# Rebuilding the end of attention and the batch norm of a conformer block

## The chip, the cores and the metric

The kernel runs on one core of one Trainium2 chip. The metric is the device time of one execution in microseconds (us). Most executions of a kernel agree within 0.3%; a change counts as faster or slower here from 2% on. The profile and the trace come from one profiled execution of each kernel; their clock starts at the span's first instruction. "Span" is the time from the first to the last instruction, some 4 us less than the device time.

## The reference

A conformer block on 2 x 4000 tokens of 512 features, bf16 inputs: feed-forward, attention, gated depthwise convolution with a batch norm over all 8000 tokens, second feed-forward, with a layer norm ahead of each and one at the end.

```python
    h = _layernorm(x, axis=-1)
    h = _silu(h @ w_ff1_a) @ w_ff1_b
    x1 = x + 0.5 * h
    ...                                        # layer norm, q, k, v
    attn = jnp.einsum('bts,bsd->btd', p, v) @ w_o
    x2 = x1 + attn
    h = _layernorm(x2, axis=-1)
    h = h @ w_pw1
    h = a * _sigmoid(b)                        # a, b: the two halves
    ...                                        # dc: depthwise, 3 taps over time
    mu = flat.mean(0)                          # over all tokens of both batches
    var = ((flat - mu) ** 2).mean(0)
    dc = (dc - mu[None, None, :]) / jnp.sqrt(var[None, None, :] + 1e-05)
    h = _silu(dc) @ w_pw2
    x3 = x2 + h
    h = _layernorm(x3, axis=-1)
    h = _silu(h @ w_ff2_a) @ w_ff2_b
    x4 = x3 + 0.5 * h
    return _layernorm(x4, axis=-1)
```

The batch norm is what makes a seam: no token can go on before the last token's convolution is counted.

## The kernel before

Tokens are worked in 16 chunks of 500, each four tiles of 125. The first feed-forward of all chunks, attention of all chunks and the second feed-forward of all chunks follow each other, and TensorE is full in each. The convolution of chunks 0 to 12 is done beside attention. Between attention and the second feed-forward lies the seam: chunk 15's projection and layer norm, the gates of chunks 14 and 15, the depthwise convolutions of chunks 13 to 15 (as matmuls with diagonal matrices), the batch norm's factors, and a start of the second feed-forward.

A layer norm takes bn_stats (statistics) of each tile, then aggregates, adds eps, and takes the power -1/2 on GpSimd for all four tiles together:

```python
    def ln_aggr(self, c, sl, shift=False):
        for ti in range(TPC):
            S.op("DVE", lambda e, ti=ti: e.bn_aggr(self.mv[sl][:, ti, :], self.st[sl][:, ti, :]), ...)
        S.op("DVE", lambda e: e.tensor_scalar(self.va[sl], self.mv[sl][:, :, 1], EPS, None, ALU.add), ...)
        S.op("POOL", lambda e: e.tensor_tensor(out=self.rs[sl], in0=self.va[sl],
                                               in1=self.neghalf[0:TILE, :], op=ALU.pow), ...)
```

The seam, cut:

```python
        gate = [f for jj in range(DC) for f in (lambda jj=jj: self.conv_b(tail, jj), lambda jj=jj: self.conv_a(tail, jj))]
        for ti in range(TPC):
            gate.pop(0)()
            self.project(last, ti)             # attention's projection, and the residual on VectorE
            self.ln_stats(last, sl, ti)
        self.ln_aggr(last, sl)
        ...
        for ti in range(TPC):
            self.ln_norm(last, sl, ti, ..., "DVE")
        self.transposes_pe(1, ("DVE", "DVE"))  # four banks, four copies
        ...
        for jj in range(DC):                   # four blocks of 128 channels of chunk 15
            self.conv_b(last, jj)
            self.conv_a(last, jj)
            ...                                # depthwise, then finish(): statistics over all 16 chunks
        ...
        for t in range(2):
            for cc in range(DC):
                self.swish(t, cc)
        self.warm(16)                          # 16 matmuls whose result nobody reads
        banks = [self.sbank() for _ in all_t]
        self.pw2(0, all_t, banks)              # second pointwise of chunk 0
        for ti in all_t:
            self.pw2_residual(0, [ti], banks[ti:ti + 1])
            self.ln_stats(0, sl, ti)
        self.ln_aggr(0, sl)
        ...
        self.pw2_sum(1, all_t, ybanks)         # chunks 1 and 2: 40 matmuls beside the layer norm
        self.pw2_sum(2, all_t, [self.sbank() for _ in all_t])
        for ti in all_t:
            self.ln_norm(0, sl, ti, ..., "DVE")
        for ti in all_t:
            self.transpose_pe(ti, 0, ("DVE", "ACT")[ti % 2], ybanks[ti])
```

## Time and profile before

| | before |
|---|---|
| device time, median of 3 | 2066.26 us (2066.22 to 2067.23) |
| span of the profiled run | 2061.7 us |
| TensorE (PE) busy | 2049.0 us, 99% |
| VectorE (DVE), ScalarE (ACT), GpSimd (POOL) busy | 54%, 36%, 6% |
| the seam, from the row sums to the first matmul of the second feed-forward | 1524.21 to 1572.74, 48.53 us |

PEld is TensorE's weight load, which overlaps its matmuls. The lines of the profile, and what follows from them, are in the prediction below. DVE, ACT and POOL are the profile's names for VectorE, ScalarE and GpSimd.

### The profile page before, as it was taken

How to read it: one execution, taken by the hardware profiler on the slowest of the kernel's cores; microseconds unless marked ns; L12 is line 12 of the kernel's file. 1: busy time of each engine (PE TensorE's matmuls, PEld its weight loads, DVE VectorE, ACT ScalarE, POOL GpSimd, SP SyncE). 2: the span in 40 equal slices, each digit the busy share in tenths (PEclk: the TensorE clock that was granted, in tenths of full speed). 3: DMA queues.
4: the chain of work that ended last, by engine and by line, in shares of the span. 5: the costliest groups of instructions: out<-in, count | busy, mean ns of one | idle time of the engine just before them, and what ended most of it. 6: DMA issues, size and time to landing. Idle time of an engine off the chain costs nothing.

```text
span 2061.7 us, 24361 instructions
## 1 busy us (share of the span) xinstructions
PE 2049.0 (99%) x9642; PEld 1038.6 (50%) x9644; DVE 1104.3 (54%) x2252; ACT 745.1 (36%) x1271; POOL 130.1 (6%) x271
## 2 busy tenths in 40 slices
PE   9999999999999999999999999999999999999998
PEld 4555555554444444444444444444445555555554
DVE  4244444325556667666666666666764434434443
ACT  3433333333333333333333333333336433443432
POOL 2011100000000000000000000000010000000000
PEclk9999999999999999999999999999999999999999
DMA  7222221110000100014301010001143111111111
GB/s 178 56 61 53 60 61 49 46 49 11 16 6 23 24 16 21 19 23 113 92 13 24 18 23 16 21 18 24 55 111 92 31 31 40 32 31 40 32 31 42
DMA packets 209324, 87.73 MB, mean 43 GB/s; under 512 B 157873, under 2 KB 208692, under 8 KB 209204
## 3 DMA queue, kind: packets, MB, share of 16 engines
q1 hardware_dynamic: 208808, 85.79, 16.9%
q8 instruction: 78, 1.28, 0.3%
q14 instruction: 42, 0.34, 0.1%
q10 hardware_dynamic: 396, 0.31, 0.0%
HBM read 29.53 MB, written 19.04 MB: 24 GB/s over the span
## 4 chain that ended last, share of the span: by engine, by line
PE 98%; DVE 1%; ACT 1%; issue 0%; POOL 0%; POOLq 0%; ACTq 0%
PE s L463 55%; PE y L463 42%; DVE wff L976 0%; ACT work L493 0%; DVE work L552 0%; ACT keys L493 0%; DVE wff L910 0%; ACT wff L493 0%; DVE work L485 0%; DVE xt L634 0%; DVE work L529 0%; DVE work L983 0%; POOL work L539 0%; PE s L478 0%; DVE work L715 0%
## 5 line engine op out<-in xcount | busy, mean ns | idle before, releaser
L493 ACT ACTIVATE work<-s 128x500 bf16<-128x500 f32 (+2 forms) x1063 | 623.9, 587 | 1220.8 <-PE s L463 1218.3
L463 PE MATMUL s<-work,wff 128*128 128x500 bf16 x2560 | 627.7, 376 | 1.4 <-ACT work L493 0.8
L463 PE MATMUL s<-work,keys 128*128 128x500 bf16 x2048 | 517.5, 374 | 0.1
L463 PE MATMUL y<-work,keys 128*128 128x500 bf16 x2048 | 514.4, 373 | 0.1
L463 PE MATMUL y<-wff,work 128*125 128x512 bf16 x2016 | 506.6, 379 | 0.0
L786 DVE TENSOR_TENSOR work<-work 128x500 f32<-128x500 f32 x496 | 334.9, 675 | 287.9 <-ACT work L493 285.3
L463 PEld LDWEIGHTS s<-work,wff 128*128 128x128 bf16 x2560 | 250.1, 98 | 280.4 <-issue 1.7
L463 PEld LDWEIGHTS y<-wff,work 128*125 128x125 bf16 x2016 | 275.2, 137 | 173.5
L463 PEld LDWEIGHTS y<-work,keys 128*128 128x128 bf16 x2048 | 199.2, 97 | 234.4 <-DVE work L851 1.1
L463 PEld LDWEIGHTS s<-work,keys 128*128 128x128 bf16 x2048 | 199.8, 98 | 232.2 <-DVE work L715 0.6
L634 DVE SCALAR_TENSOR_TENSOR xt<-y,xt 125x512 bf16<-125x512 f32 x128 | 79.8, 684 | 352.4 <-PE y L463 352.4
L529 DVE BATCH_NORM_STATS2 work<-xt 125x6 f32<-125x512 bf16 x320 | 202.5, 681 | 10.4 <-DMA xt<-in_x_dram 10.0
L539 POOL TENSOR_TENSOR work<-work 125x4 f32<-125x4 f32 x78 | 79.2, 1015 | 1122.0 <-DVE work L537 1122.0
L463 PE MATMUL s<-work 128*125 128x512 bf16 (+3 forms) x544 | 138.7, 380 | 2.4 <-DVE work L1091 1.3
L552 DVE TENSOR_SCALAR work<-xt,work 125x512 bf16<-125x512 bf16 x285 | 113.2, 442 | 19.8 <-POOL work L539 16.4
L634 DVE SCALAR_TENSOR_TENSOR xt<-s,xt 125x512 bf16<-125x512 f32 x56 | 38.7, 691 | 141.6 <-PE s L463 141.6
L463 PEld LDWEIGHTS s<-work 128*125 128x125 bf16 (+2 forms) x544 | 72.5, 135 | 51.2 <-issue 5.4
L634 DVE SCALAR_TENSOR_TENSOR xt<-s,work,xt 125x512 bf16<-125x512 f32 x64 | 48.1, 751 | 32.8 <-PE s L463 32.2
L463 PE MATMUL s<-keys,work 128*128 128x500 bf16 x256 | 64.4, 376 | 0.0
L914 DVE SCALAR_TENSOR_TENSOR wff<-wff,s 128x500 bf16<-128x500 f32 x56 | 38.0, 678 | 42.2 <-PE s L463 40.2
L493 ACT ACTIVATE wff<-s 128x500 f32<-128x500 f32 x68 | 39.9, 587 | 54.3 <-PE s L463 52.2
L961 POOL COPY wff<-wff 128x1 bf16<-128x1 bf16 x56 | 10.5, 188 | 636.4 <-DVE wff L914 626.8
(79 smaller groups left out, 518.5 us busy)
## 6 DMA issues: line engine op xcount, KB each, us to landing
xt<-in_x_dram SPq DMA_DIRECT2D x15, 500.0 KB
out_dram<-work SPq DMA_DIRECT2D x15, 500.0 KB
dcvd<-wff SPq DMA_DIRECT2D x52, 125.0 KB, 1.7
keys<-dcvd SPq DMA_DIRECT2D x13, 500.0 KB, 4.5
wff<-in_w_ff_a_dram SPq DMA_DIRECT2D x16, 256.0 KB, 4.2
keys<-work SPq DMA_DIRECT2D x8, 512.0 KB, 3.6
keys<-keys SPq DMA_DIRECT2D x32, 128.0 KB, 2.1
work<-work SPq DMA_TRANSPOSE x210, 2.5
```

Source lines behind the costliest of these rows:

```text
L463: self.S.op("PE", lambda e: e.matmul(out, lhsT, rhs, start=start, stop=stop), reads=reads, writes=[bank], inc=stop if inc is None else inc)
L493: return self.S.op("ACT", lambda e: e.activation(out, in_, func, **kw), reads=reads, writes=writes)
L529: self.S.op("DVE", lambda e: e.bn_stats(self.st[sl][:, ti, :], self.XT[g]), reads=[self.bx[g]], writes=[self.b_st[sl][ti]])
L539: S.op("POOL", lambda e: e.tensor_tensor(out=self.rs[sl], in0=self.va[sl], in1=self.neghalf[0:TILE, :], op=ALU.pow), reads=self.b_va[sl] + ...
L552: self.S.op("DVE", lambda e: e.tensor_scalar(out, self.XT[g], self.mv[sl][:, ti, 0:1], self.rs[sl][:, ti:ti + 1], ALU.subtract, ALU.mult), ...
L634: self.S.op("DVE", lambda e: e.scalar_tensor_tensor(out=self.XT[g], in0=ps, scalar=scalar, in1=self.XT[g], op0=ALU.mult, op1=ALU.add), rea ...
L786: S.op("DVE", lambda e, p=p: e.tensor_tensor(out=self.acc[s], in0=self.acc[s], in1=self.P[p], op=ALU.add), reads=[self.b_P[p], self.b_acc[ ...
L914: self.S.op("DVE", lambda e: e.scalar_tensor_tensor(out=out, in0=self.th[k], scalar=1.0, in1=ps[:, 0:CHUNK], op0=ALU.add, op1=ALU.mult), r ...
L961: S.op("POOL", lambda e: e.tensor_copy(self.G[gs][:, jj, 0:1], self.G[gp][:, jj, CHUNK:CHUNK + 1]), reads=[self.b_G[gp][jj]], writes=[self ...
```

## The change

Its intent is to shorten the seam. The layer norms there run tile by tile, each tile's small operations placed behind the next tile's statistics; the first one after the batch norm reads its tokens from PSUM. The batch norm's statistics of the first 13 chunks (14 for the first channel block) are summed up during attention, as one pseudo-entry that stands for all of them. Transposes go two tiles to a bank, with one copy for both. The warming matmuls are gone, and the second pointwise is done ahead for two chunks instead of three. One block of chunk 14's gate moves into attention (`KEEP = 1`).

```diff
+    def ln_tiles(self, c, sl, prepare=None, engs=("ACT", "ACT", "ACT", "DVE"), src=None):
+        ...
+        for ti in range(TPC):
+            if prepare:
+                prepare(ti)
+            if ti:
+                self.ln_mean(sl, ti - 1)
+            self.ln_stats(c, sl, ti, src)
+            if ti:
+                self.ln_factor(sl, ti - 1)
+            if ti > 1:
+                finish(ti - 2)
+                yield ti - 2
...
+    def conv_part(self, cc):
+        S, n = self.S, self.beside(cc)
+        b = [self.b_bst[cc]]
+        S.op("DVE", lambda e: e.bn_aggr(self.mvc[:, cc, :], self.bst[:, cc, 0:n, :].rearrange("p a b -> p (a b)")),
+             reads=b, writes=[self.b_mvc[cc]])
+        S.op("DVE", lambda e: e.memset(self.bst[:, cc, n - 1, 3:4], float(n * CHUNK)), writes=b)
+        ...                                   # mean, and variance * count + eps, beside it
...
     def conv_scale(self, cc):
-        S.op("DVE", lambda e: e.bn_aggr(self.mvc[:, cc, :], self.bst[:, cc, :, :].rearrange("p a b -> p (a b)")),
+        S, k = self.S, self.beside(cc) * 6 - 3
+        S.op("DVE", lambda e: e.bn_aggr(self.mvc[:, cc, :], self.bst[:, cc, :, :].rearrange("p a b -> p (a b)")[:, k:]),
              reads=[self.b_bst[cc]], writes=[self.b_mvc[cc]])
-        S.op("DVE", lambda e: e.tensor_scalar(self.shc[:, cc:cc + 1], self.mvc[:, cc, 1:2], EPS, None, ALU.add),
-             reads=[self.b_mvc[cc]], writes=[self.b_shc[cc]])
...
         elif t == NCK - 1:
+            self.halo_left(t, jj)
             self.S.op("DVE", lambda e: e.scalar_tensor_tensor(
                 out=out, in0=ps[:, 0:CHUNK], scalar=2.0, in1=self.th[k], op0=ALU.mult, op1=ALU.mult),
                 reads=[b_ps, self.b_th[k]], writes=wr)
...
-        AHEAD = 3
...
-        self.warm(16)
...
+        AHEAD = 2
         for cc in range(DC):
-            self.swish(2, cc)
+            self.swish(1, cc)
+        self.pw2_x(0, all_t[2:], banks[2:])
+        self.pw2(0, all_t, banks, False)
+        x = [(ps[0:TILE, :], b_ps) for ps, b_ps in banks]
+        for ti in self.ln_tiles(0, self.nxt("ln", self.LN_SLOTS), None, ("ACT", "ACT", "DVE", "DVE"), x):
+            pass
         ybanks = [ybank() for _ in all_t]
+        self.pw2_x(1, all_t, ybanks)
+        self.pw2(1, all_t, ybanks, False)
...
+        x_away(1, 0, "ACT")
+        x_away(1, 1, "DVE")
+        x_away(0, 0, "ACT")
+        for k in range(2):
+            self.transpose_pair(k, 0, ("ACT", "DVE")[k], ybanks[k])
```

The layer norm at the kernel's very start (`head`) uses the same new routine.

## The prediction

> **What bounds the kernel now.** I read the page first, its busy shares and its chain:
>
> ```profile
> PE 2049.0 (99%) x9642; PEld 1038.6 (50%) x9644; DVE 1104.3 (54%) x2252; ACT 745.1 (36%) x1271; POOL 130.1 (6%) x271
> ...
> PE 98%; DVE 1%; ACT 1%; issue 0%; POOL 0%; POOLq 0%; ACTq 0%
> ```
>
> TensorE is on the chain of the work that ended last for 98% of the span, at a granted clock of 0.999. So no other engine is worth anything except where TensorE stands still or does work that nobody needs. The view of TensorE's waits, over the whole run, shows how little it stands:
>
> ```profile
> PE s L478 <- DVE work L552: 2.1, 2, 1.2
> PE s L463 <- ACT work L493: 2.0, 4, 0.8
> PE s L463 <- DVE work L1091: 1.3, 1, 1.3
> PE s L478 <- ACT work L493: 1.2, 1, 1.2
> PE s L463 <- DVE work L485: 0.6, 1, 0.6
> ```
>
> That is 7.2 us of 2061.7, of which some 3 us are the start of the kernel (the last three rows, at 1 to 11 us in the timeline). The other 4.1 us lie in the seam between attention and the second feed-forward, the part that the change rebuilds. The table by stretches, cut at my three stages (end of attention and its layer norm; last convolution chunk; batch norm, second pointwise and layer norm) has it:
>
> ```profile
> 1524.37:1540.48 16.11, 14.04 (x83) 7.41 (x82) 12.53 (x25) 5.76 (x10) 7.45 (x13) 1.00 0.31 97
> 1540.48:1553.61 13.13, 13.13 (x64) 6.06 (x62) 9.28 (x19) 8.50 (x15) 1.91 (x13) 1.00 0.13 40
> 1553.61:1572.74 19.13, 17.15 (x89) 9.98 (x88) 12.13 (x31) 15.44 (x25) 2.68 (x4) 1.00 0.63 193
> ```
>
> Columns: stretch, length, then busy time and count of PE, PEld, DVE, ACT, POOL, clock, DMA. The seam is 48.37 us long. Busy overstates TensorE's work, for a matmul's record is longer than its place in the stream. In the chain, in order of time, four 500-column matmuls take 0.85 us (0.211 each) and four of 512 columns 0.86 (0.215). Counted from the program, the seam holds: 4 last values 0.85, row sums 0.41, 16 projection 3.43, 32 + 32 first pointwise 13.5, 36 depthwise 7.6, 32 transposes 1.9, 16 warming matmuls 3.4, 16 + 40 second pointwise with its x sums 12.0. Together 43.1, so TensorE really idles about 5.2 us. The timeline of TensorE shows where:
>
> ```profile
> 1537.10 1.03 PE L478 MATMUL s<-work 125*128 125x125 bf16 x12 [1.20 <-DVE work L552]
> 1538.99 0.38 PE L478 MATMUL s<-work 125*128 125x125 bf16 x4 [0.87 <-DVE work L552]
> ...
> 1553.61 3.54 PE L463 MATMUL s<-work 128*128 128x500 bf16 x16
> 1557.85 0.40 PE L463 MATMUL s<-work 128*125 128x512 bf16 x1 [0.70 <-ACT work L493]
> ...
> 1572.74 4.41 PE L463 MATMUL s<-work,wff 128*128 128x500 bf16 x20 [0.81 <-ACT work L493]
> ```
>
> The x16 is the warming: 3.4 us of no use, which covers the batch norm's end. Ceiling of the change: 5.2 idle + 3.4 warming + a little, about 9 us or 0.45%. A result beyond 2% is out of reach either way, unless something breaks.
>
> **What the Trainium skill says.** "Perfetto Trace Analysis", Identifying the Most-Contended Engine: matmul busy share does not measure the distance to the roofline; agreed, 99% busy hides the warming. "TensorE: Matmul & The Clock Gate", Back-to-back issue gap: N/2.4 + 2.5 ns, which is 211 and 216 ns; the trace's 0.211 and 0.215 agree (the page's other figure, 131 ns for 512 columns, does not show here). "ScalarE: Activation LUTs", What ACT_TABLE_LOAD costs: an ACTIVATE takes 186 ns + 0.833 N, each pointer operand 93 more, and neighbours overlap by 93. For 500 elements that is 0.60 and, with two pointers, 0.79; traced 0.585 and 0.790. "VectorE: DVE Perf Modes", Why PSUM operands drop a tier: an fp32 PSUM operand runs at 1x. Traced: normalising a bf16 tile from SBUF 0.41, reading fp32 from PSUM 0.63 to 0.69 (other operations; no norm from PSUM is traced yet).
>
> **The change, part by part.** TensorE loses 16 warming matmuls (3.4) and one depthwise group (3 x 0.211 = 0.63, done on VectorE in attention instead). Eight identity matmuls stay eight. Two groups of the first pointwise (8 x 0.211 = 1.69) move out of the seam into attention, and the second pointwise of chunk 2 (16 x 0.215 = 3.44) moves into the first feed-forward chunk; both places are full on TensorE, so these two moves save nothing. Total work falls by 4.0 us. What remains is the idle time, for which I walk the new order of each engine from the trace's durations, on the clock of before.
>
> Stage 1, from 1524.37. TensorE has its matmuls done and could transpose from 1534.9. VectorE sets the pace: residual 0.75, bn_stats 0.69, aggregate 0.18, +eps 0.15, shift 0.16 are 1.9 a tile. The first residual starts at 1528.4, so the last shift for a ScalarE tile ends near 1535.6; ScalarE's norm (0.8) ends 1536.4; VectorE's two norms end 1536.6 and 1537.15 after the per-tile power on GpSimd (0.56). Transposes and one depthwise end 1538.1, the copy of the second pair (about 0.7 for 1000 elements, from 0.42 for 500) ends 1538.3, ScalarE's (186 + 833 ns, 1.0 by the skill's formula) 1538.5. The next stage starts at 1538.55 instead of 1540.48: 1.93 earlier, of which 1.69 are the 8 matmuls that left, so TensorE still idles about 2.2 here (2.4 before), now for ScalarE's second norm. I take 0.41 for a VectorE norm although four of them took 3.21 us at 1535.63, because GpSimd's gates ran beside those; at 1568.77, with GpSimd idle, four took 1.38, and the change moves the last gate to VectorE, behind the norms.
>
> Stage 2. TensorE-bound with small waits: 0.05 for a bank, then about 0.3 at the last depthwise, whose bank waits for a copy behind the table load (1.28). TensorE reaches the second pointwise at 1552.2.
>
> Stage 3. The old aggregate over 16 chunks is 0.59; over the pre-summed ones I estimate 0.2, and the +eps (0.15) is gone, from each of four chains. The last swish still needs: bn_stats of the two last depthwise, aggregate, power 0.56, shift 0.15, near 1554.1; two ScalarE copies and two swishes (0.7 apart) put the third swish at 1554.3, so 0.45 of idle there; chunk 0's second pointwise ends 1556.06. Then the dominant term. Layer norm of chunk 0 read from PSUM: first statistics at 1555.6, 1.13 a tile (the period of the same tile-wise sequence at the kernel's start, bn_stats at 4.58, 5.71, 6.82), last statistics end 1559.7, powers to 1561.15, two VectorE norms to 1561.9, one copy of x out of the bank that the second pair needs (0.65) to 1562.6, transposes 1563.1, pair copy 1564.0. TensorE has only 20 matmuls (4.3) and 16 transposes (1.0) to lay beside it, where before 40 stood, so it idles some 2.5 to 3 us.
>
> The feed-forward thus starts near 1564.0 instead of 1572.74: 8.7 less, minus 3.44 and 1.69 of moved work, is 3.6 us saved. Check by the other sum: 4.0 less work, 5.2 of idle become about 5.6.
>
> Everything else I take as neutral. The head runs the same routine two tiles behind instead of one; its VectorE norm still waits for the fourth power, and the third ScalarE norm still stands behind the copy at 8.42, so 0 +- 0.2. Attention gets the gate of (14,0) and four partial sums on VectorE, which is busy 79.93 of 120 us there.
>
> **Rivals.** First: the waits win. The layer norm of chunk 0 is exposed, and the per-tile chains on three engines can slip by one semaphore each. If its idle is 5 instead of 2.7, the saving falls to 1 us (2065). For: 0.81 idle even with 40 matmuls beside. Against: it is only 1.13 a tile. Second: the overlap is better than my walk, the author's order leaving only the 2 us of pair copy and first norm: 5.5 to 6 saved (2060.5). Third: the feed-forward weights come late. 4 MB have to land after the last convolution; the stretch 1553.61 to 1572.74 moved 193 GB/s on average and 310 at its peak. 2.8 MB from about 1553 at 310 GB/s end near 1562, and the second matrix is first used four groups (3.4) after 1564, so I hold it hidden; if not, 1 to 4 us lost (2064 to 2067). Fourth: attention's last chunk becomes bound by VectorE; it has about 1 us free in each 1.69 us step and gets some 4 us over ten steps, so no.
>
> **Range and chances.** 2066.26 - 3.6 = 2062.7. The walk has some 30 handovers of which perhaps ten matter; I give it +-1.5, the rivals and 0.5 us of scatter the rest: 2060.2 to 2065.0. Beyond 2% either way would take 41 us, more than the whole ceiling.
>
> **What would show it.** No warming matmuls, and 19 TensorE instructions fewer. In the seam TensorE waits for ScalarE's first norms (about 1.5), a swish (0.4) and, before the first feed-forward matmul, for the second pair's copy, with 2.5 to 3 us of idle after the second pointwise of chunk 1. The aggregate of the batch norm at 0.2 instead of 0.59. I am wrong in the mechanism if TensorE waits for a weight transfer, or if attention or the feed-forward (pitch 0.211 and 0.215) change.

## The result, and the profile after

| | before | after |
|---|---|---|
| device time, median of 4 runs each | 2066.45 us (2066.22 to 2067.23) | 2060.96 us (2060.79 to 2061.51) |
| span of the profiled run | 2061.7 | 2056.9 |
| row sums start, first matmul of the second feed-forward | 1524.21, 1572.74 | 1525.16, 1564.25 |
| the seam between them | 48.53 | 39.09 |
| from there to the end | 488.96 | 492.65 |

The ratio is 0.9973, with a 95% interval of 0.9956 to 0.9990: within 2%, and 5.5 us less by the medians. Ratios are the mean time of one kernel's fast runs over that of the other's of the same rounds, so not quite the ratio of the medians quoted. A second set of runs gave 2060.99 against 2065.87 (4 and 7 runs, ratio 0.9976).

The page of the changed kernel, its busy shares and its chain by engine, as shown for before:

```profile
PE 2044.4 (99%) x9625; PEld 1036.1 (50%) x9625; DVE 1111.3 (54%) x2274; ACT 744.6 (36%) x1270; POOL 128.1 (6%) x275
...
PE 96%; DVE 2%; SPq 1%; DMA 1%; issue 0%; POOL 0%; ACT 0%; POOLq 0%; DVEq 0%; ACTq 0%
```

TensorE lost 4.6 us of busy time and is still 99% busy. Over the whole run the chain is still TensorE; SPq and DMA stand in it because it now starts along the queue of the loads, up to the landing of the depthwise taps at 46.28, just ahead of TensorE's matmuls of 46.33. In the seam alone VectorE had 16.9 of the chain's 48.5 us before and has 21.0 of 39.1 now: more of the seam hangs on VectorE. (9625 TensorE records instead of 9642 is near the 19 instructions that went; some records can be missing.)

TensorE's waits over the whole run: line, releaser, total us, times, longest.

```profile
PE s L465 <- DVE work L504: 1.7, 3, 0.9
PE s L465 <- DVE work L1158: 1.2, 1, 1.2
PE s L480 <- ACT work L507: 1.1, 2, 0.8
PE y L493 <- ACT work L507: 1.0, 1, 1.0
PE s L465 <- ACT work L507: 0.8, 1, 0.8
PE y L493 <- DVE xt L504: 0.3, 1, 0.3
```

They sum to 6.1 us where before had 7.2; in the seam alone it is 3.2 instead of 4.0. So the waits fell by less than 1 us; what fell most is work: the warming. Line 504 is VectorE's copy out of PSUM, 507 every ScalarE operation.

The table by stretches, cut at the same three stages (stretch, length, then busy us and count of PE, PEld, DVE, ACT, POOL, clock, DMA share, GB/s):

```profile
1525.32:1538.91 13.59, 12.34 (x76) 6.60 (x74) 9.95 (x25) 6.88 (x11) 5.23 (x10) 1.00 0.31 98
1538.91:1552.59 13.68, 13.56 (x64) 6.19 (x64) 9.62 (x19) 8.69 (x16) 3.27 (x17) 1.00 0.21 64
1552.59:1564.25 11.66, 9.48 (x54) 5.52 (x52) 8.25 (x24) 10.32 (x18) 2.77 (x6) 1.00 0.99 307
```

The third stage is the shortened one, 11.66 instead of 19.13 us, with 35 TensorE instructions fewer: the warming, and chunk 2's second pointwise, which now lies in the feed-forward (and a few at the edges, such as the x sums of chunk 0, now in the second stage). The weights fill the DMA engines there (0.99), as they did in part before, but TensorE waits for none of them.

The timeline of TensorE, the rows that begin after a wait:

```profile
1536.96 1.07 PE L493 MATMUL y<-work 125*128 125x125 bf16 x12 [0.95 <-ACT work L507]
...
1538.91 1.86 PE L465 MATMUL s<-work,wff 128*128 128x500 bf16 x8 [0.23 <-DVE work L504]
...
1556.30 1.08 PE L465 MATMUL s<-work 128*125 128x512 bf16 x4 [0.85 <-ACT work L507]
...
1562.77 0.61 PE L493 MATMUL y<-work 125*128 125x125 bf16 x8 [0.32 <-DVE xt L504]
1564.25 4.41 PE L465 MATMUL s<-work,wff 128*128 128x500 bf16 x20 [0.87 <-DVE work L504]
```

In order: the transposes of the second tile wait for ScalarE's second norm at the end of attention; chunk 15's first pointwise for the pair's copy; the last four matmuls of chunk 0's second pointwise for the last swish; the second pair of transposes for VectorE's copy of x out of the bank that it takes; and the feed-forward for that pair's copy.

Last, the chain in order of time, inside the second stage (start, us, what). L1055 is the batch norm's aggregate, L1057 its power, L1027 the copy of the left border column of chunk 15's next block, L953 that block's gate, L1048 the statistics of a depthwise:

```profile
1545.24 0.23 DVE work L1055
...
1545.55 0.55 POOL work L1057
1546.10 0.14 POOL wff L1027
...
1546.40 0.68 DVE wff L953
...
1547.14 0.60 DVE wff L1048
...
1548.49 0.26 DVE work L1055
...
1549.67 0.68 DVE wff L953
```

This is a ring of VectorE, GpSimd and TensorE (whose depthwise lies between a gate and its statistics), one turn per channel block: 1546.40 to 1549.67 is 3.27 us, where TensorE's own work per block is 14 matmuls, 2.96. In this view TensorE is off the chain from 1543.14 to 1556.30, although it stands still for little of that time. The change makes it: the left border is now copied before the gate, and it stands in GpSimd's queue behind the previous block's power, which waits for the aggregate. The gate therefore waits for a power that it has nothing to do with. No run takes the copy out of the ring; bn_late, below, makes each turn longer.

**The account.** Between the two traces: to the row sums +0.95, in the seam -9.44, after it +3.69; together -4.80, which is the difference of the spans. Work moved out of the seam is +1.69 (8 matmuls into attention) and +3.44 (16 into the feed-forward). So the seam itself is worth -9.44 + 1.69 + 3.44 = -4.31 us. The rest, -0.49, is the start of the kernel (0.88 earlier, below) less 0.39 of small differences in the two long stages.

### The profile page after: what moved, and what is told of

Its sections match the earlier page's. It is cut to its first block, busy times and chain, and to the rows that moved or that the text cites. A ratio compares the mean times of both kernels' runs of the same rounds, so it can differ in the third digit from the quotient of the medians.

```text
span 2056.9 us, 24335 instructions
## 1 busy us (share of the span) xinstructions
PE 2044.4 (99%) x9625; PEld 1036.1 (50%) x9625; DVE 1111.3 (54%) x2274; ACT 744.6 (36%) x1270; POOL 128.1 (6%) x275
## 4 chain that ended last, share of the span: by engine, by line
PE 96%; DVE 2%; SPq 1%; DMA 1%; issue 0%; POOL 0%; ACT 0%; POOLq 0%; DVEq 0%; ACTq 0%
PE s L465 54%; PE y L465 42%; SPq L515 1%; DMA xt<-in_x_dram 1%; DMA work<-in_dw_dram 0%; DVE work L547 0%; SPq L511 0%; DVE work L569 0%; DVE wff L1048 0%; DVE xt L667 0%; SPq L519 0%; POOL work L661 0%; POOL work L1057 0%; DVE wff L953 0%; ACT work L507 0%
## 5 line engine op out<-in xcount | busy, mean ns | idle before, releaser
L465 PE MATMUL s<-work 128*125 128x512 bf16 (+3 forms) x528 | 133.7, 378 | 2.2 <-DVE work L1158 1.2
L957 DVE SCALAR_TENSOR_TENSOR wff<-wff,s 128x500 bf16<-128x500 f32 x57 | 38.6, 678 | 43.5 <-PE s L465 41.4
L507 ACT ACTIVATE work<-keys,work 128x500 bf16<-128x500 bf16 x64 | 50.5, 795 | 1.1 <-DVE work L1062 1.1
```

What stands on the lines that cost most here:

```text
L465: self.S.op("PE", lambda e: e.matmul(out, lhsT, rhs, start=start, stop=stop), reads=reads, writes=[bank], inc=stop if inc is None else inc)
L507: return self.S.op("ACT", lambda e: e.activation(out, in_, func, **kw), reads=reads, writes=writes)
L957: self.S.op("DVE", lambda e: e.scalar_tensor_tensor(out=out, in0=self.th[k], scalar=1.0, in1=ps[:, 0:CHUNK], op0=ALU.add, op1=ALU.mult), r ...
```

## The experiments

Each is the changed kernel with one edit, unless it says otherwise. "Seam" is always from the row sums' first matmul to the second feed-forward's first matmul in the timeline of TensorE. (The 38.9 of the first expectations starts 0.16 us later, at 1525.32.) It repeats to 0.01 us in traces of an unchanged seam, so it tells more than times that scatter by 1 us or more. Against before, every time in the table is within 2%, and so is every difference between two rows.

| run | seam | against after | device time, median (runs) |
|---|---|---|---|
| after | 39.09 | | 2060.96 (4) |
| after_again | 39.08 | -0.01 | 2060.99 (4) |
| head_old | 39.09 | 0 | 2061.73 (4) |
| head_old_again | 39.09 | 0 | 2061.21 (5) |
| ln_seq | 39.44 | +0.35 | 2061.40 (4) |
| warm_back | 41.92 | +2.83 | 2064.00 (4) |
| bn_late | 42.31 | +3.22 | 2063.89 (4) |
| keep0 (wrong result) | 42.65 | +3.56 | 2062.97 (4) |
| keep0_fixed | 41.44 | +2.35 | 2062.12 (4) |
| shift_later | 38.39 | -0.70 | 2060.33 (4) |
| sh_scalar | 38.63 | -0.46 | 2060.71 (4) |
| best | 37.47 | -1.62 | 2059.24 (6) |
| head_new (before, edited) | 48.53 | | 2065.07 (5) |

### The start of the kernel

after_again has no edit.

> The changed kernel once more, for the scatter of its first 11 us. In the one trace of it the warming matmuls at the start became fast at 4.9 us and the first feed-forward matmul started at 10.10; in the trace of before at 7.4 and 10.98. Theory A (the new order of the layer norm at the start gains 0.9 us): first feed-forward matmul near 10.1 again. Theory B (only the moment differs at which TensorE becomes fast): anything from 10.1 to 11. Seam, from the row sums to the first matmul of the second feed-forward, 38.9 as before under both. Time 2061.0.

The first feed-forward matmul started at 10.09, so theory A stood so far. head_old puts the old order back at the start:

```diff
-        for ti in self.ln_tiles(0, 0):
-            if ti:
-                self.transpose_pe(ti - 1, 0, "ACT", banks[ti - 1])
+        for ti in range(TPC):
+            self.ln_stats(0, 0, ti)
+            if ti:
+                finish(ti - 1)
+            self.ln_mean(0, ti)
+            self.ln_factor(0, ti)
+        finish(TPC - 1)
```

> The changed kernel with the old order of the layer norm at the kernel's start (one tile behind, mean and factor straight after the statistics). Theory A (the new order there gained 0.9 us): first feed-forward matmul at 10.9 to 11.0, time 2061.8. Theory B (the clock's moment alone): as in the changed kernel, 10.1 when TensorE turns fast by 5 us, 11.0 when it turns fast at 7.4, time within 0.4 of 2061.0. Seam 38.9 in both.

It started at 10.09 too, with the old order: theory A falls as an account of the 0.88. The same kernel later, head_old_again:

> The changed kernel with the old order at its start, more rounds than the first time (which gave 2060.7 to 2065.0 in 4 runs). Theory A: median near 2062, 0.5 to 1.2 above the changed kernel, with scatter over 2 us. Theory B: 2060.5 to 2061.5, as the changed kernel.

This time it started at 11.00. The timeline of TensorE of that run, the 18 warming matmuls and the first of the feed-forward:

```profile
1.25 6.93 PE L465 MATMUL s<-work 128*128 128x500 bf16 x18 [1.25 <-DVE work L1174]
...
11.00 2.29 PE L465 MATMUL s<-work,wff 128*128 128x500 bf16 x10 [0.61 <-DVE work L504]
```

And the same two rows of the changed kernel:

```profile
1.25 5.71 PE L465 MATMUL s<-work 128*128 128x500 bf16 x18 [1.25 <-DVE work L1158]
...
10.10 3.14 PE L465 MATMUL s<-work,wff 128*128 128x500 bf16 x14 [0.61 <-DVE work L504]
```

How long the 18 matmuls take decides it, and that changes from run to run of one kernel: 5.68 us and a start at 10.09, 5.98 and 10.09, 6.17 and 10.24, 6.50 and 10.57, 6.91 (before) and 10.98, 6.93 and 11.00. The order of the layer norm does not matter to it: with a long warming the new order starts late too (6.84 and 10.91, in shift_later), and with a short one the old order starts early (5.68 and 10.09, in head_old). The Trainium skill, "TensorE: Matmul & The Clock Gate", section What's actually happening, says that the clock is released by a free-running activity window of about 3.4 us, so that the moment varies from run to run; these traces agree, with warming matmuls 0.41 us apart at first and 0.21 from a moment on, which came between about 4.0 (head_new, best) and 7.4 us (before). That is more than the 500 ns either way that the page gives.

The converse is the kernel before with the new order at its start, head_new:

> The kernel before with only the order of the layer norm at its start taken from the change. So far the spans are 60.9 to 64.4 (over 2000) of before in 15 runs, 56.4 to 58.1 of the changed kernel in 8, 56.8 to 61.0 with the old start in 4; the seam explains 4.3 us of a mean difference near 5.1. Theory A (the new start gains the rest in the mean and takes scatter away): median 0.5 to 1.2 below before of the same rounds. Theory B (the start's order is neutral, the rest is chance: the moment TensorE turns fast, and a wait for the small load of the depthwise taps near 48 us): within 0.4 of before, same scatter.

Its warming took 5.32, its feed-forward started at 10.03, and its median is 1.28 below that of before in the same rounds (ratio 0.9996, 0.9981 to 1.0011). By times alone this speaks for A; head_old_again, 0.2 above the changed kernel, speaks for B, and so do all traces of the start. Before has scattered from 2064.8 to 2068.2 in these rounds, so a median of five is worth little here. That the new order makes no difference by itself when the warming takes about equally long is shown by the traces above. Why the times of before lie about 1 us higher than the seam explains, and scatter more, is open: no slow run of before was traced. One other source of scatter was seen, a wait of 1.77 us at 48 us in sh_scalar's trace for the 3 KB load of the depthwise taps (0.52 in warm_back, none in most).

### ln_seq: where mean and factor stand in the layer norm of chunk 0

```diff
             self.ln_stats(c, sl, ti, src)
-            if ti:
+            if src:
+                self.ln_mean(sl, ti)
+                self.ln_factor(sl, ti)
+            elif ti:
                 self.ln_factor(sl, ti - 1)
```
(and the mean ahead of the statistics only where `src` is not given)

> The changed kernel with mean and factor of each tile straight after its statistics in the layer norm of chunk 0 after the batch norm (still two tiles behind with the norm). My prediction took 1.13 us a tile from the old order; the trace of after has 0.80. Theory A (the new place of mean and factor, behind the next tile's statistics start, is what makes a tile 0.80): bn_stats of that layer norm start 1.1 apart, the seam grows by 0.8 to 1.1 us (39.7 to 40.0), time +0.9. Theory B (the period is set by something else, such as reading from PSUM): 0.80 stays and nothing moves.

The timeline of VectorE in this run, statistics of tiles 1 and 2:

```profile
1557.57 0.69 DVE L547 BATCH_NORM_STATS2 work<-s 125x6 f32<-125x512 f32 x1
...
1558.59 0.69 DVE L547 BATCH_NORM_STATS2 work<-s 125x6 f32<-125x512 f32 x1
```

The same rows of the changed kernel:

```profile
1557.60 0.67 DVE L547 BATCH_NORM_STATS2 work<-s 125x6 f32<-125x512 f32 x1
...
1558.40 0.67 DVE L547 BATCH_NORM_STATS2 work<-s 125x6 f32<-125x512 f32 x1
```

1.02 us apart instead of 0.80, with the same operations. Theory A holds for the period. In the changed kernel bn_stats at 1557.60 starts 0.08 us before the aggregate ahead of it, of another tile, has ended; in ln_seq each operation needs the one just before it, and the aggregate behind the bn_stats of 1557.57 starts at 1558.30, 0.04 after its end. head_old shows the same at the kernel's start, where the prediction had its 1.13 from: with the old order bn_stats start at 4.54, 5.66 and 6.76, in the changed kernel at 4.43, 5.23 and 6.02. For the end theory A's size was too large: the seam grew by 0.35. In the changed kernel VectorE, being quicker with the statistics, then waits 0.31 for GpSimd's power before its first norm; in ln_seq it does not wait.

### warm_back: the 16 warming matmuls

```diff
+        ps, b_ps = self.Yb[1], self.b_Y[1]
+        for k in range(16):
+            self.mm(ps[:, 0:CHUNK], self.zero[:, 0:128], self.zero, True, True, [self.b_zero], b_ps, inc=k == 15)
         self.pw2(0, all_t, banks, False)
```

> The changed kernel with the 16 warming matmuls put back ahead of the second pointwise of chunk 0. They take 3.4 us of TensorE. Theory A (they were pure cost, less what TensorE would have waited for the last swish): the wait of 0.85 us vanishes, the second pointwise ends later by 2.5 to 3.1 us, and all behind it: time +2.5 to +3.1. Theory B (the last swish and the chain through the layer norm set the end whatever TensorE does before): under +1.5. Theory C (without warming TensorE's clock falls behind the seam, so warming pays): no slower, feed-forward pitch lower.

Timeline of TensorE:

```profile
1553.63 3.55 PE L465 MATMUL y<-work 128*128 128x500 bf16 x16 [0.46 <-ACT keys L507]
1557.02 3.62 PE L465 MATMUL s<-work 128*125 128x512 bf16 x16
```

The warming runs for 3.4 us, after 0.46 of waiting for its bank, and the second pointwise behind it no longer waits for any swish. The seam is 2.83 longer, in the range of theory A; B and C fall. So taking the warming away gave about 2.8 of the 4.3 us, or by estimate 2.4 if the 0.46, a wait for the bank chosen in this run, is not counted. It is not the whole 3.4 because TensorE now waits for what the warming used to cover.

### bn_late: the batch norm's statistics summed at the end

`conv_part` is not called, and `conv_scale` is that of before: an aggregate over all 16 chunks, +eps, power.

> The changed kernel with the batch norm's statistics summed only at the end, over all 16 chunks, with the separate +eps operation, as in before. Per block of channels the aggregate is 0.59 instead of 0.25 and 0.15 is added, so 0.49 a block. Theory A (the pre-summing shortens the chain from the last depthwise to the last swish, which TensorE waits for): the wait before the last four matmuls of chunk 0's second pointwise grows from 0.85 by 0.5 (only the last block counts) to 1.0 (VectorE's queue carries the third block's too), and the seam by the same; time +0.5 to +1.0. Theory B (VectorE has slack there): seam unchanged at 39.1, counted from the row sums to the first matmul of the second feed-forward.

Both theories fail, in size: +3.22. The shift of the last channel block came 2.1 us later, counted from the row sums (32.2 instead of 30.1), which is four times the 0.5 of one block. The cause is the ring shown above: aggregate, power, border, gate, statistics, aggregate are in series, so every block's 0.5 counts and not only the last one's: in the chain of this run the gates start at 1546.90 and 1550.70, 3.80 us a turn instead of 3.27. What remains, 1.1, has another cause. The table by stretches of this run (columns as above):

```profile
1557.00:1561.00 4.00, 2.62 (x7) 1.48 (x8) 2.27 (x7) 3.47 (x6) 0.74 (x2) 0.72 0.77 247
```

and its timeline of TensorE:

```profile
1558.38 1.60 PE L465 MATMUL s<-work 128*125 128x512 bf16 x4 [1.95 <-ACT work L507]
1559.77 1.91 PE L465 MATMUL y<-xt,work 125*125 125x512 bf16 x4
1561.48 3.99 PE L465 MATMUL y<-work 128*125 128x512 bf16 x16
```

After a wait of 1.95 us the granted clock, the third number from the right, is 0.72 of full speed on average, and four matmuls took 1.39 and then 1.71 us instead of 0.86. Cut finer, the same trace has it at 0.50 from 1558.80 for 3.4 us, and at 1.00 before and after. So here the wait was paid twice. That a wait of this length always is, is not shown: in sh_scalar's trace one of 1.77 us at 48 us left the clock at 1.00, and in bn_late two shorter ones (0.82 and 0.24) lay in the 8 us ahead. The changed kernel's trace has no wait over 0.95 in the seam, and a clock of 1.00 in all three stretches; the pre-summing keeps the one before the last swish at 0.85. Whether the warming of before was there to guard against the drop, or was worth its time there, no run tests: none takes it out of before. By this run the pre-summing is worth 3.2 us within the new order, and by the medians 2.9.

### keep0 and keep0_fixed: nothing of chunk 14 in attention

keep0 sets `KEEP = 0` and adds the missing depthwise of chunk 13.

> The changed kernel with nothing of chunk 14's gate done in attention: the 8 matmuls of the first pointwise return to the seam, and one depthwise group (3 matmuls, 0.63 us) returns to TensorE. Theory A (TensorE-bound, the move of the 8 is neutral): seam 39.1 + 1.7 + 0.6 = 41.4, the time to the row sums 1.7 less, time +0.6. Theory B (the 8 matmuls would also fill TensorE's 0.95 us wait for ScalarE's norm at the end of attention): seam 40.4 to 40.9, time -0.3 to +0.1. Theory C (more gates on GpSimd ahead of the norm's powers and ScalarE's copies delay the norm): time +1 or more.

Its result was wrong (relative error 0.03). I had put one depthwise of chunk 13 behind the gate of chunk 15 that overwrites its input, and that place also made TensorE wait 0.97 us. It says nothing of the change. Mended:

```diff
-    KEEP = 1
+    KEEP = 0
...
-        drains.append(self.depthwise(tail - 1, DC - 2))
+        drains.append(self.depthwise(tail - 1, 1))
...
-                f, copy = self.depthwise(tail - 1, DC - 1)
-                f()
-                copies.append(copy)
+                for cc in (DC - 2, DC - 1):
+                    f, copy = self.depthwise(tail - 1, cc)
+                    f()
+                    copies.append(copy)
```

> The run with nothing of chunk 14 done in attention, mended: in the first one a depthwise of chunk 13 stood behind the gate of chunk 15 that overwrites its input, so its result was wrong. There the seam was 42.65, with 0.97 us of wait at that depthwise. Now, by theory A (TensorE-bound: 1.7 moved, 0.63 more work) seam 41.4, time +0.6; by theory B (fills the 0.95 us wait) seam 40.4 to 40.9; by theory C (more on GpSimd, ScalarE and in the chain of the norm) seam 42 or more, time +1.2 or more.

The seam is 41.44, as theory A said to 0.04: 1.69 of work moved and 0.63 more of it. The wait for ScalarE's second norm is still 0.95; more matmuls ahead of it do not fill it, because the residuals that lead to that norm start behind the same matmuls (the first starts 5.81 us after the row sums instead of 4.11). Time +1.2 by the medians, of which theory A accounts for 0.6; that is the time that theory C stated, but its seam of 42 or more did not come, and the seam decides here.

### shift_later: one small operation out of the way

```diff
-        self.conv_shift(DC - 2)
-        self.swish(0, 2)
...
                 copies.append(copy)
+                if cc == DC - 1 and t == last:
+                    self.conv_shift(DC - 2)
+                    self.swish(0, 2)
```

> The changed kernel with VectorE's shift of the third channel block placed behind the first of the last two bn_stats, so that VectorE does not stand still 0.73 us for GpSimd's power with bn_stats waiting behind it. Theory A (that stall is on the chain to the last swish): the last swish starts 0.7 to 0.9 earlier, TensorE's wait of 0.85 falls to 0.1 or less, the seam shrinks from 39.1 to 38.3, time -0.8. Theory B (the third swish moves later by as much, or ScalarE's copies set it): under 0.3.

```profile
1556.24 1.08 PE L465 MATMUL s<-work 128*125 128x512 bf16 x4 [0.16 <-ACT work L507]
```

In this timeline of TensorE the wait for the last swish is 0.16 instead of 0.85, and the seam 0.70 shorter. Theory A holds. In the changed kernel VectorE's queue had stood 0.73 us for GpSimd's power of the third block while the statistics of the fourth were ready to be taken.

### sh_scalar: an operation with one tensor operand instead of two

```diff
-                S.op("DVE", lambda e: e.scalar_tensor_tensor(
-                    out=self.sh[sl][:, ti:ti + 1], in0=self.mv[sl][:, ti, 0:1], scalar=-1.0,
-                    in1=self.rs[sl][:, ti:ti + 1], op0=ALU.mult, op1=ALU.mult),
+                S.op("DVE", lambda e: e.tensor_scalar(
+                    self.sh[sl][:, ti:ti + 1], self.mv[sl][:, ti, 0:1], self.rs[sl][:, ti:ti + 1], -1.0,
+                    ALU.mult, ALU.mult),
```

> The changed kernel with the layer norm's shift computed by a tensor_scalar (one tensor and a pointer scalar) in place of a scalar_tensor_tensor with two SBUF tensors. In the trace of after the first shift at the end of attention took 0.74 us for one element a partition; it ended when GpSimd's gate ended, and others take 0.15. Theory A (VectorE's second SBUF input waits for GpSimd's tensor_tensor): the shift takes 0.15, VectorE's row of work at the end of attention and TensorE's 0.95 us wait for ScalarE's second norm shrink by 0.4 to 0.6, the seam falls to about 38.6, time -0.5. Theory B (the 0.74 is the wait for GpSimd's power of that tile, which no form of the operation escapes): no change.

The first shift in the changed kernel, in its timeline of VectorE:

```profile
1533.80 0.74 DVE L620 SCALAR_TENSOR_TENSOR work<-work 125x1 f32<-125x1 f32 x1
```

and GpSimd's gate in its timeline of GpSimd:

```profile
1533.29 1.25 POOL L943 TENSOR_TENSOR wff<-wff 128x500 bf16<-128x500 f32 x1 [0.21 <-ACT wff L507]
```

The same two in sh_scalar:

```profile
1535.94 0.20 DVE L620 TENSOR_SCALAR work<-work 125x1 f32<-125x1 f32 x1
```

```profile
1535.42 1.25 POOL L943 TENSOR_TENSOR wff<-wff 128x500 bf16<-128x500 f32 x1 [0.21 <-ACT wff L507]
```

In both runs GpSimd's gate is under way at that moment: 1533.29 to 1534.54 in the changed kernel, 1535.42 to 1536.67 here. GpSimd's power for that tile, theory B's suspect, had ended before the shift began in both (1532.53 and 1534.66, 0.56 each). With two SBUF tensors the operation ended when the gate did; with one tensor and a pointer scalar it took 0.20. The wait for ScalarE's second norm fell from 0.95 to 0.56 and the seam by 0.46. Theory A holds. The Trainium skill, "VectorE: DVE Perf Modes", section Two Vector instructions with no wait between them, says in its definition of read2 that what an operation reads as its second SBUF tensor goes through an interface shared with GpSimd; the two runs fit that.

### best: three edits together

shift_later, sh_scalar, and:

```diff
         x_away(1, 0, "ACT")
-        x_away(1, 1, "DVE")
         x_away(0, 0, "ACT")
         for k in range(2):
-            self.transpose_pair(k, 0, ("ACT", "DVE")[k], ybanks[k])
+            self.transpose_pair(k, 0, ("ACT", "DVE")[k], (ybanks[0], banks[0])[k])
-        for t, ti, eng in ((0, 1, "ACT"), ...
+        for t, ti, eng in ((1, 1, "DVE"), (0, 1, "ACT"), ...
```

> The changed kernel with three edits: the shift of the third channel block behind the first of the last two bn_stats (0.70 alone), the layer norm's shift as a tensor_scalar (0.46 alone), and the second pair of transposes of chunk 0 into the bank that held chunk 0's first tile, so that VectorE's copy of x (0.68) is no longer between its last norm and those transposes. If the three add up, with 0.4 for the third: seam 39.1 - 1.55 = 37.5, time 2059.4, 1.5 below the changed kernel. If the third only moves the wait to ScalarE's copies: seam 37.9. If they overlap: seam 38.2 or more.

```profile
1560.50 0.61 PE L493 MATMUL y<-work 125*128 125x125 bf16 x8
1560.99 0.61 PE L493 MATMUL s<-work 125*128 125x125 bf16 x8
1562.47 3.77 PE L465 MATMUL s<-work,wff 128*128 128x500 bf16 x17 [0.87 <-DVE work L504]
```

In this timeline of TensorE the second pair of transposes follows the first without a wait. The seam is 37.47, as expected: the three edits add up, if the third, which was not run alone, is worth the 0.4 put down for it (0.46 is left for it). The median is 2059.24 us, 1.7 below the changed kernel (five runs from 2058.82 to 2059.79, and one of 2063.48), with a correct result. The ratio to before of its rounds is 0.9971 (0.9957 to 0.9984); that one run lifts its mean.

## Why the prediction was right or wrong

Within 2% was right, and 2060.96 lies in the range of 2060.2 to 2065.0. The gain was larger than stated: 5.5 us by the medians and 4.3 in the seam alone, against 3.6. About 1 us of the 5.5 lies outside the seam, where the prediction saw nothing. By its own steps, from the row sums on (predicted, measured):

- **Ceiling and bound.** Right. TensorE's pitch and both long stages are unchanged, apart from the moved work, and the total of waits hardly fell (7.2 to 6.1).
- **Moved work is neutral.** Right: keep0_fixed shows it for the 8 matmuls (41.44 against 41.4, and 1.58 us less between the first feed-forward matmul and the row sums), and the time after the seam grew by 3.69 for the 16, predicted 3.44.
- **Stage 1 starts the next stage 1.93 earlier.** Measured 2.52 (16.27 to 13.75 us behind the row sums). The mechanism was right, TensorE waits for ScalarE's second norm. The mis-sized term is "1.9 a tile" on VectorE: a tile took 1.45 (residuals at 1530.92 and 1532.37), except the one with the blocked shift, 2.10. The 1.9 is the sum of the records' lengths, as if each operation waited for the one before it; in the new order they overlap (the aggregate starts 0.66 after a residual whose record lasts 0.75). The blocked shift, 0.74 instead of 0.16, was not foreseen; sh_scalar shows what it is.
- **Stage 2 is TensorE-bound.** Its length was right, 13.65 predicted and 13.68 measured, but its reading was incomplete. The prediction took the gates as free to start; in fact the new border copy puts them into a ring with GpSimd's powers of 3.27 us a block, just slower than TensorE's 2.96. TensorE itself waited only 0.29 there, at the last depthwise, for a copy behind the table load, as predicted (0.3); the ring costs in the next step.
- **The last swish: 0.45 of idle.** Chunk 0's second pointwise took 4.62 from its start instead of 3.86, so with 3.44 of work the idle is 1.18 by the prediction's count (the 0.85 of the view begins only at the end of the last record). The wait stood before the matmuls of the fourth swish, not of the third. The failed term is "near 1554.1" for the last shift, 15.55 after the start of stage 2, where 16.33 was measured (1538.91 to 1555.24): the ring and the shift that stalls for a power (shift_later, 0.70 of it) made it late. Counted from the row sums it was hardly late, 30.1 against 29.9: what TensorE gained in stage 1 it gave back here as waiting. The aggregate went from 0.59 to 0.26, predicted 0.2.
- **Layer norm of chunk 0: 7.94 from the end of that pointwise to the feed-forward.** Measured 7.04 (1557.21 to 1564.25). The failed term is "1.13 a tile (the period of the same tile-wise sequence at the kernel's start)". It is not the same sequence: the change places mean and factor behind the next tile's statistics, and the period is 0.80. head_old shows that the order makes this difference at the start, and ln_seq 0.22 of it a tile here; the rest of 1.13 is in part the shift (0.08), which the old order puts into each period. The other links, from the last statistics to the feed-forward, took 4.38 against 4.3 as walked, though a norm read from PSUM, which no trace had shown, took 0.77 where one from SBUF takes 0.41. TensorE's idle behind the second pointwise of chunk 1 was of the predicted kind, about 1.8 us instead of 2.5 to 3.
- **The sum.** 14.34 + 13.65 + 3.86 + 7.94 = 39.79 predicted, 13.75 + 13.68 + 4.62 + 7.04 = 39.09 measured. The misses are -0.59, +0.03, +0.76 and -0.90. That the sum is off by only 0.7 is in part luck: the third cancels most of the first or the last. The first and the last are of one kind, operations on VectorE taken as if each waited for the one before it.
- **The head is neutral.** Right as far as the order of instructions goes (10.09 with either order when the warming is short, 10.9 to 11.0 with either when it is long). Its +-0.2 was too small for the chance in when the clock rises, which moves the first feed-forward matmul by 0.9. The last 1 us of difference in the times is not explained by any trace; head_new and head_old_again disagree on whether the start's order has a part in it.
- **Rivals.** Waits did not win. The second rival, a better overlap (5.5 to 6 saved, 2060.5), came nearer in time than the prediction's own 2062.7; in the seam, where it would have to show, 4.31 were saved, between the two. Weights arrived in time: no wait of TensorE in the seam is for a load. Attention's last chunk was not bound by VectorE: up to the row sums the trace is 0.95 longer, which is the moved 1.69 less the 0.88 of the start, and 0.14.

## What to carry to other kernels

When one engine is full nearly everywhere, count its work in the few stretches where it is not, and ask what each useless instruction there was covering before taking it out: here 16 warming matmuls were worth 2.8 of their 3.4 us, in a kernel whose chain behind them had been shortened too (without the pre-summing, 3.2 us are lost again, more than the 2.8). On an in-order engine, put between an operation and its user one that depends on neither, and look at what stands in front of an operation in another engine's queue: a border copy behind an unrelated power tied three engines into a ring. A duration that a trace has for the old order of operations is not the duration of a new order.

## What the Trainium skill lacked or had wrong

- "VectorE: DVE Perf Modes", Rules for kernel authors, says to minimise the number of operations, since the drain between them comes regardless; The DRAIN you can't avoid adds that an operation that is not held starts earlier. What the order of operations is worth is in neither section: the same bn_stats, aggregate and +eps took 1.02 us a tile with dependents next to each other and 0.80 with them apart.
- "TensorE: Matmul & The Clock Gate", Why this matters for your kernels, advises no idle gaps over about 3 us. In bn_late one wait of 1.95 us was followed by matmuls at half pace (0.43 us instead of 0.215) and a granted clock of 0.50 for 3.4 us; one of 1.77 us in sh_scalar was not.
- The same page, Back-to-back issue gap, gives 131 ns a matmul of 512 columns for a sustained stream; in the trace of before four of 512 columns take 0.86 us, 215 ns each.
- "GPSIMD Engine Reference" has no duration for a power of one element per partition, which is on every chain here: 0.55 us, and 1.02 for four.
